# First block of a fused attention and mixture-of-experts kernel: a list order for its attention, half-slot conversion, another ring for one buffer

## The chip, the core and the metric

The kernel runs on one core of a Trainium2 chip. The metric is device time in microseconds of one execution; three executions of the kernel before are at hand, and one more was profiled. Engines are called PE (TensorE), DVE (VectorE), ACT (ScalarE), POOL (GpSimd) and SP (SyncE, which only issues the DMAs here).

## The reference

What is computed, cut to what matters (B, H, S, D = 8, 8, 576, 64; 4608 tokens of 512 features; 2048 hidden features; 8 experts):

```python
q_s = softmax(q, axis=-1); k_s = softmax(k, axis=2)          # k: over the sequence
kv  = einsum('bhsd,bhse->bhde', k_s, v)
x   = einsum('bhsd,bhde->bhse', q_s, kv)                     # -> x[4608, 512]
r   = maximum(x @ w_in, 0); x = (s * r * r + b) @ w_out      # w_in, w_out arrive as 8-byte floats
out = gate(x) * (relu(x @ w1[e]) @ w2[e])                    # e: each token's best expert
```

## The kernel before

The kernel has two parts. The first runs over 12 blocks of 384 tokens (index t) and within a block over 16 slots (index m). Slot m of block t issues the first product of 128 hidden features (`emit_l1`, lines 426 to 428, 12 matmuls, called L1), the activation of the slot before (`emit_g`, on ACT), and the second product of two slots before (`emit_l2`, called L2). Block 0 alone does L2 in full precision for all but its last two slots (L462), reading the joined weight; later products use a high and a low part (L464 to L466). The second part of the kernel is the expert product over sorted tokens; nothing in it is touched.

Two kinds of other work are woven into the slots as Python generators, one step of each per half slot: before L1 (first half) and after L2 (second half).

The attention. A K job (`attn_k`) takes one batch and one pair of heads: maxima over the sequence on DVE (L218 to L225), a transpose on PE (L229), a reduction on DVE (L232), a transpose on PE that spreads it (L235), a subtraction on DVE (L254, L256), Exp on ACT (L261, L262), ten matmuls with v on PE (L270), the division on DVE (L276 to L278), and a high and a low part of the result (`kvh` on ACT, L284; `kvl` on DVE, L287). A Q job (`attn_q`) takes one block and one pair of heads: row maxima on DVE (L298), six Exp on ACT (L333 in block 0, L364 in block 1), the division on DVE (L337 to L340), three transposes on PE (L347), a copy on ACT (L349), the output matmul with `kv` on PE (L352), and a high part on ACT (`xth`, L355) and a low part on DVE (`xtl`, L356). Each job of block 0 ends in loading (through SP) the data of the job that will use its buffers next: k and v at the division, q at `xth`.

The weights. The two weight matrices arrive as 8-byte floats in 16 pairs of 128-row groups of 1 MB each, in the order in0, in1, out0, in2, out1, ... in7, out6, out7. `conv_load` issues a pair's two DMAs; `conv_a` scales the upper words on ACT (Abs, L147) and takes the lowest bits and the sign on DVE (L148, L149); `conv_b` joins them on DVE (L156) and writes the high part on ACT (L160); `conv_c` subtracts on DVE (L164). The joined pair lives in a ring of two buffers for each matrix (`cxin`, `cxout`), `ct` has one buffer, and L462 reads the joined pair of w_out directly. `conv_step` does, in one go: the load of pair i+4, `conv_b` of pair i-1, `conv_a` of pair i, `conv_c` of pair i-1.

What sets the order. The program runs under a manual schedule: each engine executes its instructions in the order in which the Python code issues them, and waits are put in by the framework. Ahead of slot 0 there are 16 head steps (`for c in range(-16, 0)`), in each of which every active job advances by one step; `plan_k` and `plan_q` hold the half slot at which each job starts, and `conv_step` runs at head steps -16 and -7. In block 0, `conv_step` runs ahead of L1, twice in slot 0. PSUM has three rings: `ps_h` (2 banks, L1), `ps_y` (3 banks, L2) and `ps_a` (3 banks, all of the attention). SP issues loads in program order as well.

The loads ahead of the head are issued in this order (w is one weight pair, k, q and v the four head pairs of block 0):

```python
for w in "q0 k0 w k1 q1 q2 v0 k2 v2 k3 q3 v1 w v3 w".split():
```

Of the kernel before, what the change touches and what calls it, by code (L numbers as in the profile page):

```python
# [11 lines left out]
I32 = mybir.dt.int32  # L12
# [13 lines left out]
NM = DFF // 128  # L26
# [10 lines left out]
KP = 1  # L37
# [5 lines left out]
def attn_ffn_moe(ctx: ExitStack, tc: tile.TileContext, q, k, v, w_in, w_out, s_in, b_in,  # L43
                 emb, tau, w1, w2, out, ysc=None):
# [23 lines left out]
    def ps_a():  # L68
        return ps.tile([128, 512], F32, tag="a", name="ps_a", bufs=3)
# [69 lines left out]
    def conv_a(kind, i):  # L139

        t = sp.tile([128, 1024], I32, tag="ct", name="ct", bufs=1)
        x = sp.tile([128, 1024], I32, tag="cx" + kind, name="cx" + kind)
        raw = raw_t.pop((kind, i)).rearrange("p n c -> p (n c)")
        r = raw.rearrange("p (f two) -> p f two", two=2)
        r16 = raw.bitcast(U16).rearrange("p (f four) -> p f four", four=4)
        x16 = x.bitcast(U16).rearrange("p (f two) -> p f two", two=2)
        nc.scalar.activation(out=t.bitcast(F32), in_=r[:, :, 1].bitcast(F32), func=AF.Abs, scale=2.0 ** -112)  # L147
        nc.vector.tensor_scalar(out=x, in0=r[:, :, 0], scalar1=29, scalar2=None, op0=ALU.logical_shift_right)  # L148
        nc.vector.tensor_scalar(out=x16[:, :, 1], in0=r16[:, :, 3], scalar1=0x8000, scalar2=None,  # L149
                                op0=ALU.bitwise_and)  # L150
        conv_t[kind, i] = (t, x)
# [61 lines left out]
    def attn_k(b, j, kt, vt, dg, after=None, ke=None):  # L213
# [11 lines left out]
        nc.vector.tensor_tensor(out=d2[0:64], in0=d2[0:64], in1=k4[0:64, :, 4, :], op=ALU.max)  # L225
        yield
        if b <= KP:
            pt = ps_a()
            nc.tensor.transpose(pt[:, 0:128], dg, ident)  # L229
# [3 lines left out]
            yield  # L233
            pb = ps_a()
            nc.tensor.transpose(pb[:, 0:128], cm.to_broadcast([128, 128]), ident)  # L235
# [20 lines left out]
        nc.vector.tensor_tensor(out=k4[0:64, :, 4, :], in0=k4[0:64, :, 4, :], in1=mb[0:64], op=ALU.subtract)  # L256
        if b > KP:
            yield
# [5 lines left out]
        if b > KP:  # L264
            yield
        pk = ps_a()
        for r in range(5):
# [16 lines left out]
        nc.scalar.activation(out=kvh[b % 2][:, j, :], in_=dg, func=AF.Copy)  # L284
        if b > KP:
            yield
# [14 lines left out]
    def attn_q(t, j, qt, after=None, qe=None):  # L301
        i = t % 2
# [25 lines left out]
        elif t == 0:  # L328
# [6 lines left out]
            yield  # L335
            yield
            nc.vector.tensor_scalar(out=qr, in0=qr, scalar1=1e-9, scalar2=None, op0=ALU.add)  # L337
# [8 lines left out]
            for r in range(NC):  # L346
# [7 lines left out]
            after()  # L354
            nc.scalar.activation(out=xth[0][:, j, :], in_=px[:, 0:BT], func=AF.Copy)  # L355
            nc.vector.tensor_tensor(out=xtl[0][:, j, :], in0=px[:, 0:BT], in1=xth[0][:, j, :].bitcast(F32),  # L356
                                    op=ALU.subtract)
# [483 lines left out]
    with tc.manual_schedule():  # L841
# [10 lines left out]
        for i in range(NP):  # L852
            if i + 1 < NP:
# [4 lines left out]
                 "v": lambda j: load_v(0, j, v0[j])}  # L858
        for w in "q0 k0 w k1 q1 q2 v0 k2 v2 k3 q3 v1 w v3 w".split():
            if w == "w":  # L860
                conv_load(*loads.pop(0))
            else:
                load0[w[0]](int(w[1]))
        nc.sync.dma_start(out=s_sb, in_=s_in.partition_broadcast(128))
        nc.sync.dma_start(out=b_sb, in_=b_in.partition_broadcast(128))
        conv_load(*loads.pop(0))
        conv_i = [0]

        def conv_step():

            i = conv_i[0]
            if i >= len(order) + 1:
                return
            if loads:
                conv_load(*loads.pop(0))
            if i > 0:
                conv_b(*order[i - 1])
            if i < len(order):
                conv_a(*order[i])
            if i > 0:  # L880
                conv_c(*order[i - 1])
            conv_i[0] += 1

# [9 lines left out]
        for j in range(4):  # L893
            plan_k.append((2 * j - 16, 0, j, k0[j], v0[j], d0[j]))
            plan_q.append(((0, 2, 4, 7)[j] - 16, 0, j, q0[j]))
        for b, sl in enumerate(((-4, 4, 12, 22), (28, 40, 52, 63), (75, 87, 98, 109), (120, 132, 144, 156),
                                (168, 180, 191, 203), (216, 228, 240, 252), (264, 276, 287, 299)), start=1):
            for j in range(4):
                plan_k.append((sl[j], b, j, kt_s, vt_s, dg_s))
        for j, sl in enumerate((-2, 6, 12, 22)):  # L900
            plan_q.append((sl, 1, j, qt_s))
# [25 lines left out]

        for c in range(-16, 0):
            start_pairs(c)
            run(act)  # L930
            if c in (-16, -7):
                conv_step()
        start.close()
# [74 lines left out]
        for t in range(NB):  # L1008
            for m in range(NM + (LAG if t == NB - 1 else 0)):
# [13 lines left out]
                if t == 0:  # L1023
                    next(g, None)
                    conv_step()
                    if m == 0:
                        conv_step()
                step(prep)
# [7 lines left out]
                if m < NM:  # L1036
                    start_pairs(2 * (NM * t + m) + 1)
                run(act)
                if (t, m) == (0, NM - 1):
                    assert conv_i[0] >= len(order) + 1  # L1040
                    consts_late()
                    late_open()
# [139 lines left out]
```

## Time and profile before

| | us |
|---|---|
| median of three runs (lowest, highest) | 1409.32 (1408.02, 1411.92) |
| profiled execution | 1407.17 |
| its span, first to last instruction | 1405.4 |
| busy in the span: PE, DVE, ACT, POOL | 1338.8, 1008.0, 889.4, 173.1 |
| mean granted clock of PE, share of full speed | 0.983 |

The page's shares of busy time are means over the whole span. The change concerns the first tenth of it, so the views to read are those by stretch: windows with each engine's busy time, the waits (who waited for whom, and for how long), and the timeline, whose rows give start and length of each instruction and in brackets how long its engine stood idle ahead of it and what released it.

### The profile page before, as it was taken

What the parts mean: (1) busy time and instruction counts of PE and PEld (TensorE: products, weight loads), DVE (VectorE), ACT (ScalarE), POOL (GpSimd) and SP (SyncE); (2) the same over time, 40 slices, a digit from 0 to 9 for tenths busy, and PEclk for the clock granted to TensorE, in tenths of its full rate; (3) what the DMA queues carried; (4) which work ended last, traced back from release to release, by engine and by line L of the source; (5) the groups of instructions that cost most, each with busy time, mean ns of one, the idle gap of its engine ahead of it and who ended that gap; (6) DMA issues with size and microseconds to landing.
All of it is one profiled execution on the core that took longest, in us unless ns stands there. A gap on an engine that the chain in (4) does not pass through costs nothing. (4 is left out here: it accounts for less than half of the span.)

```text
span 1405.4 us, 22783 instructions
## 1 busy us (share of the span) xinstructions
PE 1338.8 (95%) x7650; PEld 1181.1 (84%) x7650; DVE 1008.0 (72%) x2589; ACT 889.4 (63%) x1767; POOL 173.1 (12%) x170
## 2 busy tenths in 40 slices
PE   4898999999999999999999999998999999999995
PEld 2666888888888889888989988987888989899994
DVE  6886797878696969596969593647777666666642
ACT  5776767777676776677777675664554555555542
POOL 0000000000000000000010100113533221212110
PEclk9899999999999999999999999999999999999998
DMA  8641412121211121212111000412222222523332
GB/s 274 221 164 31 124 38 51 37 56 29 57 40 51 30 68 29 51 29 63 35 46 29 27 20 15 159 38 61 68 64 65 69 69 73 190 69 129 128 110 73
DMA packets 107456, 104.72 MB, mean 75 GB/s; under 512 B 55105, under 2 KB 83521, under 8 KB 107331
## 3 DMA queue, kind: packets, MB, share of 16 engines
q1 hardware_dynamic: 100098, 83.74, 20.3%
q0 software_dynamic: 7232, 19.44, 4.2%
q8 instruction: 62, 1.02, 0.3%
q14 instruction: 64, 0.52, 0.2%
HBM read 141.07 MB, written 19.73 MB: 114 GB/s over the span
## 5 line engine op out<-in xcount | busy, mean ns | idle before, releaser
L426 PE MATMUL ps_h<-xth,win 128*128 128x384 f32 x768 | 266.8, 347 | 0.8 <-ACT r L439 0.8
L427 PE MATMUL ps_h<-xtl,win 128*128 128x384 f32 x768 | 261.1, 340 | 0.0
L428 PE MATMUL ps_h<-xth,win 128*128 128x384 f32 x768 | 260.8, 340 | 0.0
L465 PE MATMUL ps_y<-wout,gl 128*128 128x512 f32 x534 | 210.9, 395 | 1.1 <-DVE gl L449 1.1
L466 PE MATMUL ps_y<-wout,gh 128*128 128x512 f32 x534 | 211.6, 396 | 0.0
L464 PE MATMUL ps_y<-wout,gh 128*128 128x512 f32 x534 | 210.0, 393 | 0.0
L654 DVE TENSOR_TENSOR l<-r,h 128x1024 fp32r<-128x1024 f32 x143 | 174.5, 1238 | 20.1 <-ACT h L653 17.4
L541 DVE CUSTOM_DVE_ANT_0 scr<-ysb,eb 128x512 bf16<-128x512 f32 x264 | 181.7, 688 | 5.8
L690 PE MATMUL ps_h<-xh,l 128*128 128x256 f32 x576 | 166.5, 289 | 7.5 <-DVE l L654 7.4
L449 DVE TENSOR_TENSOR gl<-r,gh 128x384 fp32r<-128x384 f32 x178 | 97.9, 550 | 100.9 <-ACT gh L447 98.9
L688 PE MATMUL ps_h<-xh,h 128*128 128x256 f32 x576 | 165.4, 287 | 2.6 <-ACT xh L664 1.8
L689 PE MATMUL ps_h<-xh,h 128*128 128x256 f32 x576 | 165.5, 287 | 1.1 <-DVE xh L665 1.1
L653 ACT ACTIVATE h<-r 128x1024 fp32r<-128x1024 f32 x152 | 155.7, 1050 | 0.0
L426 PEld LDWEIGHTS ps_h<-xth,win 128*128 128x128 f32 x768 | 145.6, 190 | 9.2 <-ACT r L439 1.6
L427 PEld LDWEIGHTS ps_h<-xtl,win 128*128 128x128 f32 x768 | 145.6, 190 | 5.3 <-issue 0.5
L428 PEld LDWEIGHTS ps_h<-xth,win 128*128 128x128 f32 x768 | 145.4, 189 | 0.0
L439 ACT ACTIVATE r<-ps_h 128x384 f32<-128x384 f32 x192 | 93.7, 488 | 80.5 <-PE ps_h L428 69.3
L446 ACT ACTIVATE r<-r,b_sb,s_sb 128x384 f32<-128x384 f32 x178 | 126.3, 709 | 5.9
L705 DVE SCALAR_TENSOR_TENSOR hl<-ps_h,hh 128x512 fp32r<-128x512 f32 x76 | 52.5, 691 | 104.5 <-ACT hh L704 94.0
L704 ACT ACTIVATE hh<-ps_h 128x512 fp32r<-128x512 f32 x76 | 45.4, 597 | 129.4 <-PE ps_h L690 117.1
L690 PEld LDWEIGHTS ps_h<-xh,l 128*128 128x128 f32 x576 | 112.7, 196 | 9.8 <-DVE l L654 9.8
L466 PEld LDWEIGHTS ps_y<-wout,gh 128*128 128x128 f32 x534 | 100.3, 188 | 23.0
(264 smaller groups left out, 2505.3 us busy)
## 6 DMA issues: line engine op xcount, KB each, us to landing
r<-moe_w SPq DMA_DIRECT2D x156, 512.0 KB
ysc<-ysb SPq DMA_DIRECT2D x36, 256.0 KB
x<-xr SPq DMA_DIRECT2D x288, 32.0 KB
qt_s<-q SPq DMA_DIRECT2D x45, 192.0 KB
rawin<-moe_w_in SPq DMA_DIRECT2D x16, 512.0 KB
rawout<-moe_w_out SPq DMA_DIRECT2D x16, 512.0 KB
kt_s<-k SPq DMA_DIRECT2D x29, 256.0 KB
vt_s<-v SPq DMA_DIRECT2D x29, 256.0 KB
```

The source lines that it names most:

```text
L426: nc.tensor.matmul(hp, wh[:, ws], xth[i][:, kk, :], start=(kk == 0), stop=False)
L427: nc.tensor.matmul(hp, wh[:, ws], xtl[i][:, kk, :], start=False, stop=False)
L428: nc.tensor.matmul(hp, wl[:, ws], xth[i][:, kk, :], start=False, stop=(kk == KC - 1))
L464: nc.tensor.matmul(y, g[:, cs], wh, start=(m == 0), stop=False)
L465: nc.tensor.matmul(y, l[:, cs], wh, start=False, stop=False)
L466: nc.tensor.matmul(y, g[:, cs], wl, start=False, stop=(m == NM - 1))
L541: nc.vector.tensor_tensor_reduce(out=junk_box[-1], in0=yt, in1=eb[:, e, :], scale=1.0, scalar=0.0, op0=ALU.mult, op1=ALU.add, accum_out=dt ...
L653: nc.scalar.activation(out=hi, in_=raw, func=AF.Copy)
L654: (eng or nc.vector).tensor_tensor(out=lo, in0=raw, in1=hi.bitcast(F32), op=ALU.subtract)
L688: nc.tensor.matmul(o, wh, xh[:, kk, :], start=(kk == 0), stop=False)
L689: nc.tensor.matmul(o, wh, xl[:, kk, :], start=False, stop=False)
L690: nc.tensor.matmul(o, wl, xh[:, kk, :], start=False, stop=(kk == KC - 1))
```

## The change

- The head is no longer 16 rounds over all jobs, but one list that names, entry by entry, the job whose next step is issued: k0 to k3 and q0 to q3 of block 0, c (a generator that converts in0), K and Q (the first jobs of the next batch and block, begun in the list), and w (a weight load). Two steps of K and two of Q are issued in the list, where four and two were issued in the head before.
- For the list, the jobs of block 0 get further `yield`s, so that each step of theirs is on one engine: between subtraction and Exp, and between `kvh` and `kvl` in `attn_k`, between `xth` and `xtl` in `attn_q`, where also an empty step goes.
- The K jobs of block 0 take their PSUM banks from `ps_y`, which L2 doesn't use yet; Q stays on `ps_a`.
- The first loads are in another order, with the first weight pair behind q2 instead of behind k0, the second one last; the third and fourth are issued in the list.
- `conv_step` is cut into two halves. The first, ahead of L1, issues the load and `conv_b`; the second, behind the slot's second attention step, issues `conv_a` of the next pair and `conv_c`. A pair is finished one slot later than before.
- The joined pair out7 gets its buffer from the ring of w_in.
- Some jobs of later batches and blocks start at other half slots.

```diff
     def conv_a(kind, i):
...
-        x = sp.tile([128, 1024], I32, tag="cx" + kind, name="cx" + kind)
+        room = "in" if (kind, i) == ("out", NM // 2 - 1) else kind
+        x = sp.tile([128, 1024], I32, tag="cx" + room, name="cx" + kind)
...
+        bank = ps_y if b == 0 else ps_a
         if b <= KP:
-            pt = ps_a()
+            pt = bank()
...
-            pb = ps_a()
+            pb = bank()
...
-        if b > KP:
+        if b > KP or b == 0:
             yield
         e = kt if ke is None else ke()
...
-        pk = ps_a()
+        pk = bank()
...
         nc.scalar.activation(out=kvh[b % 2][:, j, :], in_=dg, func=AF.Copy)
-        if b > KP:
+        if b > KP or b == 0:
             yield
...
             yield
-            yield
             nc.vector.tensor_scalar(out=qr, in0=qr, scalar1=1e-9, scalar2=None, op0=ALU.add)
...
             nc.scalar.activation(out=xth[0][:, j, :], in_=px[:, 0:BT], func=AF.Copy)
+            yield
...
-        for w in "q0 k0 w k1 q1 q2 v0 k2 v2 k3 q3 v1 w v3 w".split():
+        for w in "q0 k0 k1 q1 v0 k2 q2 w v1 k3 q3 v2 v3 w".split():
...
-        conv_load(*loads.pop(0))
-        conv_i = [0]
-
-        def conv_step():
+        conv_i = [1]
+
+        def conv_first():
+            yield
+            conv_a(*order[0])
+            yield
+            conv_b(*order[0])
+            yield
+            yield
+            conv_c(*order[0])
+
+        def conv_step(half):
 
             i = conv_i[0]
-            if i >= len(order) + 1:
+            if i > len(order):
                 return
-            if loads:
-                conv_load(*loads.pop(0))
-            if i > 0:
-                conv_b(*order[i - 1])
-            if i < len(order):
-                conv_a(*order[i])
-            if i > 0:
-                conv_c(*order[i - 1])
-            conv_i[0] += 1
+            if half == 0:
+                if loads:
+                    conv_load(*loads.pop(0))
+                if i > 1:
+                    conv_b(*order[i - 1])
+            else:
+                if i < len(order):
+                    conv_a(*order[i])
+                if i > 1:
+                    conv_c(*order[i - 1])
+                conv_i[0] += 1
...
-            plan_k.append((2 * j - 16, 0, j, k0[j], v0[j], d0[j]))
-            plan_q.append(((0, 2, 4, 7)[j] - 16, 0, j, q0[j]))
-        for b, sl in enumerate(((-4, 4, 12, 22), (28, 40, 52, 63), (75, 87, 98, 109), (120, 132, 144, 156),
+            plan_k.append((-16, 0, j, k0[j], v0[j], d0[j]))
+            plan_q.append((-16, 0, j, q0[j]))
+        for b, sl in enumerate(((-2, 6, 14, 22), (30, 41, 52, 63), (75, 87, 98, 109), (120, 132, 144, 156),
...
-        for j, sl in enumerate((-2, 6, 12, 22)):
+        for j, sl in enumerate((-2, 6, 14, 22)):
...
-        for c in range(-16, 0):
-            start_pairs(c)
-            run(act)
-            if c in (-16, -7):
-                conv_step()
+        start_pairs(-16)
+        line = {f"{w}{j}": act[4 * i + j] for i, w in enumerate("kq") for j in range(4)}
+        line["c"] = conv_first()
+        act.clear()
+        start_pairs(-2)
+        line["K"], line["Q"] = act
+        for w in ("q0 q0 k0 k1 k0 k0 k1 q0 k0 k0 q0 q0 k1 q1 k0 k1 k2 q1 k0 k1 k2 k2 k1 q2 k2 q1 q2 k2 q1 k0 c q2 "
+                  "k1 q1 k3 q2 k2 q0 c q2 k3 q0 w w k2 k0 q3 c q3 k3 k1 c q3 k3 q1 k1 k3 q3 q1 c k3 q3 k3 k2 q0 k2 k3 "
+                  "q2 q1 k3 q2 k0 K q3 q3 q2 K q3 Q Q k1 k2 k3").split():
+            if w == "w":
+                conv_load(*loads.pop(0))
+            else:
+                next(line[w], None)
...
+        conv_step(0)
+        conv_step(1)
...
                 if t == 0:
                     next(g, None)
-                    conv_step()
-                    if m == 0:
-                        conv_step()
+                    conv_step(0)
...
                 run(act)
+                if t == 0:
+                    conv_step(1)
```

## Rows read from the trace of the kernel before

**Rows 1.** Windows by stage: us, busy us (instructions) by engine, granted clock, DMA share, rate.

```profile
core 0: us, PE busy (x) PEld busy (x) DVE busy (x) ACT busy (x) POOL busy (x), PEclk, DMA share, GB/s
...
4.76:40.08 35.32, 18.89 (x110) 10.99 (x111) 24.95 (x71) 20.16 (x72) 0.00 (x0) 0.87 0.96 308
40.08:58.46 18.38, 15.12 (x73) 12.55 (x74) 17.08 (x29) 13.56 (x29) 0.00 (x0) 0.79 0.76 257
58.46:102.99 44.53, 42.11 (x208) 29.41 (x207) 38.30 (x64) 36.65 (x78) 1.11 (x4) 1.00 0.47 157
102.99:135.34 32.35, 27.52 (x123) 19.42 (x122) 21.65 (x47) 20.37 (x43) 3.14 (x7) 0.95 0.13 34
135.34:1405.40 1270.06, 1235.12 (x7144) 1108.67 (x7142) 906.02 (x2381) 798.64 (x1548) 166.84 (x144) 0.99 0.22 63
```

**Rows 2.** Waits of PE, 40 to 136 us: total, times, longest.

```profile
PE ps_a L270 <- ACT kt_s L261: 5.6, 2, 4.8
PE ps_a L235 <- DVE cm L232: 2.8, 2, 1.6
PE ps_a L379 <- DVE qt_s L371: 2.4, 1, 2.4
```

**Rows 3.** Timeline of the head: start, length, engine, line, operands [idle before <-releaser].

```profile
2.63 1.06 SPq L136 DMA_DIRECT2D rawin<-moe_w_in  x2
...
5.76 0.54 DVE L298 TENSOR_REDUCE qs<-qt_s 128x6 f32<-128x384 f32 x1
...
8.79 1.28 ACT L147 ACT_TABLE_LOAD   x1 [8.79 <-DMA rawin<-moe_w_in]
8.81 0.69 DVE L148 TENSOR_SCALAR cxin<-rawin 128x1024 int32<-128x1024 int32 x1 [2.51 <-DMA rawin<-moe_w_in]
...
10.08 1.13 ACT L147 ACTIVATE ct<-rawin 128x1024 f32<-128x1024 f32 x1
...
11.11 0.34 ACT L333 ACTIVATE qt_s<-qt_s,qs 128x64 f32<-128x64 f32 x1
```

**Rows 4.** The same view: lengths of single steps of block 0's attention.

```profile
13.23 0.17 DVE L337 TENSOR_SCALAR qr<-qr 128x6 f32<-128x6 f32 x1 [1.21 <-ACT qt_s L333]
...
14.28 0.90 PE L347 MATMUL ps_a<-ident,qe 128*128 128x128 f32 x3 [2.19 <-DVE qe L340]
...
15.80 1.56 PE L270 MATMUL ps_a<-vt_s,ke 128*64 128x66 f32 x20 [0.62 <-ACT ke L261]
...
18.50 1.62 PE L352 MATMUL ps_a<-qt_s,dg_s 128*128 128x384 f32 x2 [0.52 <-DVE dg_s L278]
...
20.24 0.28 DVE L287 TENSOR_TENSOR kvl<-dg_s,kvh 128x128 fp32r<-128x128 f32 x1
...
39.14 0.56 DVE L356 TENSOR_TENSOR xtl<-ps_a,xth 128x384 fp32r<-128x384 f32 x1 [1.70 <-ACT xth L355]
```

**Rows 5.** The same view: one weight pair's conversion on DVE.

```profile
27.91 1.22 DVE L156 SCALAR_TENSOR_TENSOR cxin<-ct,cxin 128x1024 int32<-128x1024 int32 x1
...
29.04 0.69 DVE L148 TENSOR_SCALAR cxin<-rawin 128x1024 int32<-128x1024 int32 x1
...
29.76 0.76 DVE L149 TENSOR_SCALAR cxin<-rawin 128x1024 uint16<-128x1024 uint16 x1
...
30.41 1.21 DVE L164 TENSOR_TENSOR win<-cxin,win 128x1024 fp32r<-128x1024 f32 x1
```

**Rows 6.** Timeline of PE and DVE, 115 to 127 us.

```profile
115.33 2.74 PE L462 MATMUL ps_y<-cxout,gh 128*128 128x512 f32 x6
...
118.11 0.69 DVE L148 TENSOR_SCALAR cxout<-rawout 128x1024 int32<-128x1024 int32 x1 [5.72 <-PE ps_y L462]
...
122.89 1.45 PE L270 MATMUL ps_a<-vt_s,kt_s 128*64 128x66 f32 x20 [4.83 <-ACT kt_s L261]
...
125.29 0.52 PE L427 MATMUL ps_h<-xtl,win 128*128 128x384 f32 x1
...
126.54 0.34 PE L428 MATMUL ps_h<-xth,win 128*128 128x384 f32 x1
```

More of the change, by code (lines that the diff above doesn't have):

```diff
@@ L926, in start_pairs @@
                     act.append(attn_q(t, j, qt, after=aft, qe=e))
-        for c in range(-16, 0):
-            start_pairs(c)
-            run(act)
-            if c in (-16, -7):
-                conv_step()
+        start_pairs(-16)
[11 more added lines that the diff above has]
+                next(line[w], None)
+        assert all(next(line[w], 0) == 0 for w in line if w not in "KQ")
+        conv_step(0)
+        conv_step(1)
         start.close()
@@ L1038, in attn_ffn_moe @@
                 run(act)
+                if t == 0:
+                    conv_step(1)
                 if (t, m) == (0, NM - 1):
-                    assert conv_i[0] >= len(order) + 1
+                    assert conv_i[0] > len(order)
                     consts_late()
```

## The prediction

> **What bounds the kernel now.** I read the windows by stage first [rows 1]. Their bounds are the starts of PE's L426 in slots 0, 3, 11 and 16 of the first token block (slot 16 is slot 0 of the second block), which I call L1(0), L1(3), L1(11), L1(16). From L1(16) to the end PE is busy 1235.12 of 1270.06 us: that part is bound by PE, the change doesn't touch its instructions, and it moves as a whole with the moment at which it begins. So the question is by how much L1(16), now at 135.34, moves. Before it PE is not the bound: up to L1(0) at 40.08 it has 18.89 us of work, and DVE has 24.95 us of work in a stretch of 35.32, so that DVE is idle for 10.37. In slots 3 to 10 PE is busy 42.11 of 44.53 us (5.57 a slot) with DVE close behind (38.30). In slots 11 to 15 it falls back: 27.52 of 32.35, or 6.47 a slot.
>
> Then the waits of PE between L1(0) and L1(16) [rows 2]: the longest is 4.83 us, at L270 for the exponentials of a K job. Its row [rows 6] leads back to DVE: the first step of the last weight pair (L148, out7) waited 5.72 us for the L2 matmuls that end with the row at 115.33, because its buffer was still that of out5; everything behind it in DVE's order, the attention too, waited with it. PE then came back at 1.2 GHz: a matmul of L1 lasts 0.52 us at 125.29 and 0.34 at 126.54.
>
> Last, the head in order of time [rows 3]. The row maxima of q0 end at 6.30, but the first Exp starts at 11.11: ACT stood in order behind the Abs of in0, whose megabyte was in SP's queue ahead of k1, behind its table load, and behind the Abs itself. DVE lost 2.51 us there in the same way.
>
> **The change, part by part.** No arithmetic instruction is added or removed; only orders, banks and one buffer change. I sum against the profiled execution (1407.17 us, of which 1405.4 is the span); the median, 1409.32, lies 2.15 above it, and I carry the difference over.
>
> *The head (list order, loads, own banks).* DVE's work ahead of L1(0) is 24.95 less what now comes behind it: the first two steps of in1 (0.69 + 0.76 [rows 5]), the row maxima of the next Q (0.54, priced by L298 [rows 3]), three low halves of kv (3 x 0.28 [rows 4]), and one maximum of the next K (0.28, by the same row as the nearest of its size): 21.84. The maxima of q0 (0.54) can run while k0 is still landing, so DVE ends at 4.76 + 21.30 + its waits = 26.1 + waits. Both ends for the waits: 2 us (an estimate: the last chain of output matmul, copy and difference, which nothing can cover; now it shows as the 1.70 wait of the last xtl [rows 4]) and 10.4 as now, which gives L1(0) between 28 and 36.5. Between them I stepped through the list by hand, each engine taking its steps in list order at the lengths of [rows 3 to 5]: Exp of q0 from 5 to 7 (after 1.28 of table load), kv matmuls (L270, 1.56 each) of the four pairs at 10.8, 16.2, 20.8 and 27.0, the output matmuls (L352, 1.62 each) at 18.7, 22.9, 28.5 and 30.1, one transpose, and L1(0) at 32.2. DVE's largest waits on the way are 1.4 (maximum of k2, whose transpose is behind the kv matmuls of pair 0 on PE), 2.4 (product of q3, whose exponentials are on ACT behind the copy of in0) and 0.7 (last difference); all of them together 6.1. I take 32.2: **7.9 us earlier**. In0 doesn't decide there: with 4.2 MB ahead (tile sizes) and the 308 GB/s of the window [rows 1] everything has landed by about 18, and its first use is at 18.0.
>
> *SP's queue.* The loads of out0 and in2 now stand behind the loads for the next K and Q, and these wait for kv matmul 0 and output matmul 0 (20.3 above). Two more megabytes at 308 GB/s land by 28; their first steps come at 38 and 43. Nothing is late by 10 us; cost zero, and if that cover were gone each us of lateness would cost one.
>
> *K and Q of the next block, two steps less in the head.* The maximum and the second transpose of K move into slot 0, where PE has no L2 yet: nothing on the path. Stepping on from 32.2, L1(1) and L1(2) start at 36.5 and 44.4 and L1(3) at 50.3, 18.1 after L1(0) against 18.38 now: **-0.3**.
>
> *Half slots.* The step that joins the two parts of a weight (L156) now stands at the head of a slot and waits for an Abs issued half a slot before; behind it in DVE's order stand the second half's attention steps, the next pair's shift and mask, and the difference L164. In slots where six Exp (11.11 to 13.23, 2.1 us [rows 3, 4]) stand ahead of the Abs on ACT, L156 waits about 1.3; elsewhere the waits of L156 and L164 go under. The trace has no such order, so I bound it: as now, 5.57 a slot (8 slots: 0), or by stepping, 23.0 us for each four slots, 5.74 a slot (8 slots: **+1.4**). Below nothing is possible too: PE idles 2.42 us in these slots [rows 1], and all of it could go. I take +0.5, nearer to the row. A weight is ready a slot later than now; in the stepping the joined out pair is there 1.9 us before the L2 that reads it and the in pair 3 us before L1, so the cover is thin, and this is a rival below.
>
> *out7 in the other ring.* Its buffer was last read by the difference of in6, three slots earlier. The 5.72 on DVE and the 4.83 on PE go, and the five slots 11 to 15 take 5.57 to 5.74 each, 27.9 to 28.7 instead of 32.35: **-3.6 to -4.5**, I take -4. Late next there is K's exponential at its normal pace. The table's fill (POOL, L118 on) now waits for the difference of out7 instead of L156; it is read much later.
>
> Sum: 7.9 + 0.3 - 0.5 + 4.0 = 11.7 us earlier. 1407.17 - 11.7 = 1395.5 for a profiled execution, **1397.6** beside the median.
>
> One rule speaks against a larger gain. The row: after the 4.83 us wait PE runs at 1.2 GHz [rows 6], and the granted clock is 0.79 over slots 0 to 2 [rows 1]. The Trainium skill, "TensorE: Matmul & The Clock Gate" (What's actually happening), says that the slow clock is the default and that activity releases it. By that rule the head, where PE is still fed in pieces, ends at 1.2 GHz and L1(0) is as slow as now; without it L1(0) would be faster by 12 x (0.52 - 0.34), about 2.2 us. My steps have the slow lengths.
>
> **The rivals.**
> 1. *The head keeps its waits.* The chains K to Q to output are as long as now, and DVE waits about as much (10.4), or the small transfers land later than I assume. For: each pair still passes DVE, PE, ACT in turn seven or eight times. Against: the 4.8 us at the start of [rows 3] go whatever follows. L1(0) at 36.5, sum -7.4: 1402.
> 2. *The conversion becomes the bound.* With one slot less of lead, PE waits for L156 or L164. If each of 16 slots costs 0.5 more, 8 us go back: 1406, no change that can be told (a measurement here tells some 0.3%, 4.2 us). Against: DVE has 6.2 us to spare in slots 3 to 10.
> 3. *Slower.* In the slots, L156 waits for the whole Abs (1.13) and L164 for the whole copy (taken as long) in every slot, since DVE takes its steps in order and can't go round either. That is 2.3 us a slot, of which the stepping has about half; another 1.1 in 16 slots is 18 us: 1415. It decides from a slot of 6.5 us on. Against: now the same chain runs in one piece, with both waits in the same half, and slots 3 to 10 take 5.57.
> 4. *More.* DVE's waits in the head fall to 2 us and the slots close up to PE's work: 4 + 2.4 more, 1391.
> 5. *The list brings nothing,* L1(0) stays at 40 behind the transfers, and only out7 counts: 1405. The 308 GB/s speaks against it; I count it with 2.
>
> **How the numbers follow.** Forecast (1394 to 1400.5) 0.60; rival 1 (1401 to 1405) 0.19; rivals 2 and 5 0.09; rival 3 0.04; rival 4 0.08. Faster by over 0.3% holds forecast, 1 and 4: 0.87; within 0.3%: 0.09; slower 0.04. The range goes from 1392 (a part of rival 4) to 1404 (most of rival 1), leaving about 0.2 out.
>
> **What would show it.** L1(0) near 32 and the first Exp before 7; no wait of L148 for ps_y; PE's waits between L1(0) and L1(16) below 5 us; L1(16) between 122 and 126. Wrong if L1(0) lies beyond 36, if slots 3 to 10 take more than 48 us in all, if PE's L426 waits for L164 or L462 for L156, or if PE gets idle time after L1(16) that it doesn't have now.

## The result and the profile after

| | before | changed kernel |
|---|---|---|
| median, us (lowest, highest, executions) | 1409.28 (1408.02, 1411.92) | 1395.84 (1395.08, 1398.78, 4) |
| ratio to before, 95% interval | | 0.9906 (0.9886 to 0.9926) |
| profiled execution, us; its span | 1407.17; 1405.4 | 1398.78; 1397.1 |

The change makes the kernel 13.4 us faster; the forecast was 1397.6 in a range of 1392 to 1404. The total came out right. Of its terms only the head's did so for the reason given, and that only up to L1(0).

First the windows by stage, as in [rows 1] (columns as there), cut at the same places: PE's first row of L1 in slots 0, 3 and 11 of block 0, and slot 0 of block 1. In the changed kernel the lines are one or two further down: L428 is the first line of L1, L464 the L2 of block 0, L272 the matmuls of a K job.

```profile
4.82:31.92 27.10, 18.41 (x109) 10.98 (x110) 21.08 (x62) 17.06 (x69) 0.00 (x0) 1.00 0.90 269
31.92:51.35 19.43, 14.13 (x74) 11.81 (x73) 16.37 (x31) 13.89 (x30) 0.00 (x0) 0.82 0.73 263
51.35:95.57 44.22, 42.75 (x208) 29.50 (x207) 37.96 (x64) 35.38 (x75) 0.00 (x0) 1.00 0.60 213
95.57:124.06 28.49, 26.42 (x124) 17.79 (x122) 23.38 (x43) 21.25 (x45) 4.62 (x10) 1.00 0.21 64
124.06:1397.10 1273.04, 1236.71 (x7142) 1110.11 (x7142) 908.50 (x2392) 799.11 (x1550) 169.80 (x144) 0.99 0.22 63
```

Against [rows 1]: L1(0) comes 8.2 us earlier (40.08 to 31.92), slots 0 to 2 take 1.05 more (18.38 to 19.43), slots 3 to 10 take 0.3 less, slots 11 to 15 take 3.9 less (32.35 to 28.49), and L1(16) comes 11.3 earlier (135.34 to 124.06). The rest, in which the change only starts one K job half a slot later, took 3.0 more in this execution (1270.06 to 1273.04), and so the profiled execution, the highest of the four, is only 8.4 below the one before. Those 3 us have a section of their own at the end.

The head, in order of time (start, length, engine, line, operands, in brackets the idle time ahead and what ended it). These rows answer to [rows 3] and [rows 4]:

```profile
3.37 1.28 ACT L335 ACT_TABLE_LOAD   x1 [3.37 <-DMA qt_s<-q]
4.67 0.35 ACT L335 ACTIVATE qt_s<-qt_s,qs 128x64 f32<-128x64 f32 x1
...
11.06 1.56 PE L272 MATMUL ps_y<-vt_s,ke 128*64 128x66 f32 x20 [0.64 <-ACT ke L263]
...
17.16 1.56 PE L272 MATMUL ps_y<-v,ke 128*64 128x66 f32 x20 [1.49 <-DMA v<-v]
...
18.09 0.42 DVE L219 TENSOR_TENSOR scr<-k 128x256 f32<-128x256 f32 x1 [0.88 <-DMA k<-k]
...
25.23 0.17 DVE L338 TENSOR_SCALAR qr<-qr 128x6 f32<-128x6 f32 x1 [2.26 <-ACT q L335]
...
31.92 0.67 PE L428 MATMUL ps_h<-xth,win 128*128 128x384 f32 x1
```

The reader is to see that the first Exp no longer stands behind in0 (4.67 instead of 11.11) and brings its table load forward with it (3.37 instead of 8.79), and that two loads are late all the same: the second v by 1.49 on PE, a k by 0.88 on DVE.

Then the waits of PE, from L1(0) to L1(16), and the longest of DVE from 0 to 124 us (line waiting, what for, total, times, longest):

```profile
PE ps_a L272 <- ACT kt_s L263: 5.6, 3, 4.5
PE ps_h L428 <- ACT r L441: 2.4, 3, 0.9
PE ps_a L237 <- DVE cm L234: 0.8, 1, 0.8
```

```profile
DVE cxin L157 <- ACT ct L148: 5.3, 4, 1.4
DVE wout L165 <- ACT wout L161: 3.8, 5, 0.8
```

PE's largest wait is again one for K's exponential, but at another place: the 4.83 of [rows 6] at the end is gone, and 4.47 stand in slot 1. The subtraction that Exp needs (L256) comes on DVE right behind a conversion's last step (L165).

```profile
40.23 1.21 DVE L165 TENSOR_TENSOR win<-cxin,win 128x1024 fp32r<-128x1024 f32 x1
...
41.36 0.67 DVE L256 TENSOR_TENSOR kt_s<-kt_s,ps_a 128x512 f32<-128x512 f32 x1
42.07 0.63 ACT L263 ACTIVATE kt_s<-kt_s 128x512 f32<-128x512 f32 x1 [1.89 <-DVE kt_s L256]
42.75 1.56 PE L272 MATMUL ps_a<-vt_s,kt_s 128*64 128x66 f32 x20 [4.47 <-ACT kt_s L263]
...
45.27 0.52 PE L429 MATMUL ps_h<-xtl,win 128*128 128x384 f32 x1
```

Behind this wait PE runs at 1.2 GHz again (0.52 for a matmul of L1, 0.34 at 2.4 GHz).

### The profile page after: what moved, and what is told of

Read it like the earlier page. It is cut to its first block, busy times and chain, and to the rows that moved or that the text cites. A ratio compares the mean times of both kernels' runs of the same rounds, so it can differ in the third digit from the quotient of the medians.

```text
span 1397.1 us, 22791 instructions
## 1 busy us (share of the span) xinstructions
PE 1338.4 (96%) x7650; PEld 1180.2 (84%) x7650; DVE 1007.8 (72%) x2589; ACT 888.1 (64%) x1767; POOL 176.4 (13%) x170
## 5 line engine op out<-in xcount | busy, mean ns | idle before, releaser
L428 PE MATMUL ps_h<-xth,win 128*128 128x384 f32 x768 | 265.9, 346 | 2.4 <-ACT r L441 2.4
L656 DVE TENSOR_TENSOR l<-r,h 128x1024 fp32r<-128x1024 f32 x143 | 174.4, 1237 | 19.7 <-ACT h L655 17.0
L428 PEld LDWEIGHTS ps_h<-xth,win 128*128 128x128 f32 x768 | 145.7, 190 | 11.2 <-ACT r L441 4.3
L468 PEld LDWEIGHTS ps_y<-wout,gh 128*128 128x128 f32 x534 | 100.3, 188 | 22.9
```

The lines of the kernel that those rows point to most:

```text
L428: nc.tensor.matmul(hp, wh[:, ws], xth[i][:, kk, :], start=(kk == 0), stop=False)
L468: nc.tensor.matmul(y, g[:, cs], wl, start=False, stop=(m == NM - 1))
L656: (eng or nc.vector).tensor_tensor(out=lo, in0=raw, in1=hi.bitcast(F32), op=ALU.subtract)
```

## Experiments

The question was which part of the change brought the 11.3 us, and whether the parts add. The changed kernel has three: the **head** (list, loads, banks, fewer steps of K and Q), the **half slots** (which are two things: one conversion less in slot 0, so that each pair is finished a slot later, and the cut of the step into two), and the **ring** of out7. Kernels were made with one part alone, with one part taken back, and with single edits inside a part.

All of them in one table. "0 to 3" is the time from L1(0) to L1(3), and so on, from the timeline of PE in each kernel's profiled execution. Ratios are to the kernel before, whose medians beside these runs were 1408.58 (first four), 1407.67 (next four) and 1407.57 (last four).

| kernel | median, us (lowest to highest, n) | ratio (95%) | L1(0) | 0 to 3 | 3 to 11 | 11 to 16 | L1(16) |
|---|---|---|---|---|---|---|---|
| before | 1409.28 | 1 | 40.1 | 18.4 | 44.5 | 32.3 | 135.3 |
| changed | 1395.84 (1395.08 to 1398.78, 4) | 0.9906 (0.9886 to 0.9926) | 31.9 | 19.4 | 44.2 | 28.5 | 124.1 |
| e1 changed, ring taken back | 1394.55 (1393.01 to 1399.67, 6) | 0.9910 (0.9894 to 0.9927) | 30.4 | 20.0 | 43.9 | 28.7 | 123.0 |
| e2 before, ring alone | 1405.41 (1401.75 to 1407.28, 11) | 0.9974 (0.9965 to 0.9983) | 40.7 | 19.5 | 44.7 | 26.8 | 131.6 |
| e3 before, half slots alone | 1400.85 (1400.23 to 1402.47, 5) | 0.9948 (0.9936 to 0.9961) | 40.5 | 13.2 | 44.9 | 27.7 | 126.4 |
| e4 before, head alone | 1407.29 (1403.8 to 1409.48, 12) | 0.9989 (0.9979 to 0.9999) | 31.7 | 22.6 | 45.1 | 33.6 | 133.0 |
| e5 changed, K on `ps_a` | 1397.27 (1394.81 to 1402.95, 6) | 0.9923 (0.9906 to 0.9940) | 33.9 | 19.8 | 43.9 | 27.9 | 125.6 |
| e6 changed, old load order | 1400.92 (1397.58 to 1402.26, 6) | 0.9949 (0.9934 to 0.9963) | 34.7 | 19.7 | 44.0 | 28.3 | 126.8 |
| e7 changed, K's four steps in the list | 1396.52 (1396.03 to 1398.5, 6) | 0.9922 (0.9910 to 0.9935) | 33.8 | 16.0 | 44.0 | 28.6 | 122.3 |
| e8 changed, in0 loaded later | 1395.84 (1394.26 to 1396.79, 5) | 0.9912 (0.9898 to 0.9926) | 31.0 | 19.0 | 44.7 | 28.3 | 122.9 |
| e9 before, one conversion less in slot 0 | 1402.75 (1399.62 to 1403.1, 5) | 0.9962 (0.9947 to 0.9977) | 41.4 | 13.4 | 46.0 | 29.9 | 130.6 |
| e10 head and e9's edit, uncut | 1398.84 (1394.73 to 1401.59, 6) | 0.9937 (0.9921 to 0.9952) | 30.6 | 19.0 | 45.0 | 29.9 | 124.5 |
| e11 e7, e8 and one list entry | 1391.42 (1388.36 to 1395.08, 5) | 0.9884 (0.9865 to 0.9903) | 30.7 | 14.4 | 45.6 | 28.3 | 119.0 |
| e12 changed, again | 1394.24 (1393.83 to 1396.42, 4) | 0.9901 (0.9883 to 0.9918) | 31.5 | 19.4 | 44.3 | 28.2 | 123.3 |

The changed kernel, e1, e4, e10 and e12 have the same head (list, loads and banks); their L1(0) lie between 30.4 and 31.9. They follow PE's wait for the second v: 30.4 where it waits for none (e1), 30.6 with 0.5 (e10), 31.5 to 31.9 with 1.5 to 1.6 (e12, e4, changed). So a difference of 1.5 us in L1(0) between two profiles can't be told from none, and one of that size in L1(16) is not relied on here either.

### The ring, taken back and alone

```diff
-        room = "in" if (kind, i) == ("out", NM // 2 - 1) else kind
-        x = sp.tile([128, 1024], I32, tag="cx" + room, name="cx" + kind)
+        x = sp.tile([128, 1024], I32, tag="cx" + kind, name="cx" + kind)
```

The lines marked - stand in the changed kernel; e1 is the changed kernel with the line marked +, e2 the kernel before with the lines marked -.

> The changed kernel with out7's joined pair back in the ring of w_out; nothing else differs. The prediction's theory (the ring takes away the 5.72 us wait, worth 4 us): 4 us slower than the changed kernel, some 1400, with L148/L149's step of out7 waiting about 5 us for L2 matmuls, and L1(16) near 128. Rival theory (the half-slot order issues that step behind the L2 that frees the buffer, one slot later than before, so the ring is not needed): within 1 us of the changed kernel, no wait of that step for ps_y over 0.5 us, L1(16) at 124 to 125.

> The kernel before, with only out7's joined pair moved to the ring of w_in. The prediction's theory: 4 us faster than before (1405), the 5.72 us wait on DVE and the 4.83 us wait on PE gone, L1(16) at 130.5 to 131.7. Rival: the wait only moves to another wait of DVE or ACT in the same slots (the conversion still ends where attention makes it end), and less than 1.5 us is gained, L1(16) beyond 133.8.

Taken back, nothing returns: e1 is as fast as the changed kernel (0.9910 and 0.9906), its slots 11 to 15 take 28.7. Alone, it does what the prediction priced: slots 11 to 15 fall from 32.3 to 26.8, L1(16) comes 3.7 earlier (in this profile L1(0) and slots 0 to 2, where out7 plays no part yet, took 1.7 more), the time falls by 3.2 us by the medians. The rows of out7's first steps (DVE, `cxout<-rawout`) and of the L2 that last reads out5, whose buffer out7 takes in the ring of w_out (PE), first of e1:

```profile
107.24 2.74 PE L463 MATMUL ps_y<-cxout,gh 128*128 128x512 f32 x6
...
109.96 1.21 DVE L156 SCALAR_TENSOR_TENSOR cxout<-ct,cxout 128x1024 int32<-128x1024 int32 x1
...
111.09 0.68 DVE L148 TENSOR_SCALAR cxout<-rawout 128x1024 int32<-128x1024 int32 x1
```

and of e2, where the lines are one further down on DVE:

```profile
114.12 0.69 DVE L149 TENSOR_SCALAR cxout<-rawout 128x1024 int32<-128x1024 int32 x1
...
117.15 2.74 PE L463 MATMUL ps_y<-cxout,gh 128*128 128x512 f32 x6
```

In e2 out7 begins 3 us before that L2 does (it runs until 119.89): there the other ring is needed. In e1 it begins 1.1 us after the L2 has ended (107.24 + 2.74 = 109.98) and waits for nothing, in the old ring. With the half slots DVE comes to out7 only after that L2 is done. So the 5.72 us of [rows 6] can be removed in two ways, and the change has both; the second is worth nothing.

### The half slots, alone

```diff
-        def conv_step():
+        def conv_step(half):
...
+            if half == 0:
+                if loads:
+                    conv_load(*loads.pop(0))
+                if i > 0:
+                    conv_b(*order[i - 1])
+            else:
+                if i < len(order):
+                    conv_a(*order[i])
+                if i > 0:
+                    conv_c(*order[i - 1])
+                conv_i[0] += 1
...
-                    conv_step()
-                    if m == 0:
-                        conv_step()
+                    conv_step(0)
...
+                if t == 0:
+                    conv_step(1)
```

> The kernel before with only the conversion cut into half slots (head as before, out7 in its own ring, a pair finished one slot later than before). The prediction's theory: slots 3 to 10 get 0 to 1.4 us longer and the end keeps its wait, so 1409 to 1411. Rival (the half-slot order frees the end by itself): the 5.72 us wait is gone, 3 to 5 us faster than before, 1404 to 1406, L1(16) at 130 to 132.

This part, which had been priced at a cost of 0.5, is the largest gain of all: 7.7 us by the medians, L1(16) 9.0 earlier. That is more than either of the two theories had. 5.2 are in slots 0 to 2 (18.38 to 13.20) and 4.6 in slots 11 to 15 (32.35 to 27.73), where out7's wait is gone as in e1; L1(0) and slots 3 to 10 took 0.8 more. What happened in slots 0 to 2 is to be seen in the timeline of the kernel before:

```profile
45.34 1.22 DVE L156 SCALAR_TENSOR_TENSOR cxout<-ct,cxout 128x1024 int32<-128x1024 int32 x1
...
47.84 1.22 DVE L164 TENSOR_TENSOR wout<-cxout,wout 128x1024 fp32r<-128x1024 f32 x1
...
49.41 0.56 DVE L371 TENSOR_TENSOR qt_s<-qt_s,qr 128x384 f32<-128x384 f32 x1
...
50.02 0.55 PE L379 MATMUL ps_a<-ident,qt_s 128*128 128x128 f32 x3 [2.41 <-DVE qt_s L371]
...
51.90 0.52 PE L427 MATMUL ps_h<-xtl,win 128*128 128x384 f32 x1
```

and of e3:

```profile
43.38 0.56 DVE L371 TENSOR_TENSOR qt_s<-qt_s,qr 128x384 f32<-128x384 f32 x1
...
47.95 0.49 PE L379 MATMUL ps_a<-ident,qt_s 128*128 128x128 f32 x3
48.20 0.42 PE L426 MATMUL ps_h<-xth,win 128*128 128x384 f32 x1
```

The window of slots 0 to 2 in e3, columns as in [rows 1]:

```profile
40.51:53.71 13.20, 13.20 (x74) 11.15 (x74) 12.21 (x23) 10.87 (x26) 0.00 (x0) 1.00 0.51 143
```

Before, a whole conversion (45.34 to 49.06) stands on DVE ahead of the product L371 that PE's transposes wait for. PE loses 2.41 there, and the slot after it runs at 1.2 GHz (0.52 at 51.90). In e3 the same product begins at 43.38, PE waits for nothing there and keeps 2.4 GHz. In the window PE is now busy all the time: of the 5.18 us, 3.26 were idle time (15.12 busy of 18.38) and 1.92 work that took longer at the lower clock. The wait is in [rows 2] (L379, 2.4), with its line and what it waited for, and the prediction went past it.

### One conversion less in slot 0, without the cut

```diff
                     conv_step()
-                    if m == 0:
-                        conv_step()
```

> The kernel before without the second whole conversion step in slot 0, so that every pair is finished one slot later, as in the changed kernel, but still in one piece ahead of L1. Theory A (the half slots win by this lag alone: slot 0 has 3.8 us of DVE work less in front of the attention, and out7's first step is issued a slot later): L1(3) at 53 to 55 as in the half-slot run, L1(16) at 126 to 128.5, 1400 to 1403. Theory B (it is the cut that wins, because the attention's steps come between the two parts): L1(3) at 57 or later, out7's step still waits 2 us or more, L1(16) beyond 131, 1405 or more.

Of the two things in the half slots this is the one that makes slots 0 to 2 short: 13.4, as in e3 (13.2). At the end out7's wait is gone too, since out7 now comes a slot later. What the cut adds to that is to be seen in the later slots: 46.0 and 29.9 here against 44.9 and 27.7 with it, 1.1 and 2.1 us, and so L1(16) is at 130.6, beyond the 128.5 of theory A. In the time the two are not told apart (1402.75 and 1400.85, the intervals overlap).

### The head, alone and with that edit

e4 is the changed kernel with out7 in its own ring and both halves of the conversion run in one go ahead of L1, twice in slot 0, as before:

```diff
                     conv_step(0)
+                    conv_step(1)
+                    if m == 0:
+                        conv_step(0)
+                        conv_step(1)
...
-                if t == 0:
-                    conv_step(1)
```

> The changed kernel's head (list order, banks of its own, order of the first loads, start slots of the jobs), with the conversion in whole steps as before and out7 in its own ring. The prediction's theory: L1(0) near 32 and L1(3) 8 us earlier than before, the 5.7 us wait at out7 as before, so 8 us faster than before: 1401. Rival (the earlier start only makes PE wait longer at out7 or in the slots, because DVE's conversion sets the end of block 0): 3 us faster or less, 1406 or more, L1(16) beyond 132.

The head alone brings L1(0) from 40.1 to 31.7, and the kernel 1.3 us by the medians (0.9989, 0.9979 to 0.9999): almost all is given back. Slots 0 to 2 take 22.6 instead of 18.4, slots 11 to 15 have out7's wait as before (33.6). The timeline of e4 behind L1(0):

```profile
37.77 0.69 DVE L148 TENSOR_SCALAR cxout<-rawout 128x1024 int32<-128x1024 int32 x1
...
40.28 1.21 DVE L156 SCALAR_TENSOR_TENSOR cxout<-ct,cxout 128x1024 int32<-128x1024 int32 x1
...
42.76 1.22 DVE L164 TENSOR_TENSOR wout<-cxout,wout 128x1024 fp32r<-128x1024 f32 x1
...
44.80 0.68 DVE L255 TENSOR_TENSOR kt_s<-kt_s,ps_a 128x512 f32<-128x512 f32 x1
...
46.20 1.57 PE L271 MATMUL ps_a<-vt_s,kt_s 128*64 128x66 f32 x20 [8.10 <-ACT kt_s L262]
```

K's subtraction (L255), two steps further back in the job than before, now stands behind two conversions on DVE, and PE waits 8.10 for its Exp. Without the second conversion in slot 0 (e10):

> The changed kernel's head with the conversion in one piece, without the second step in slot 0, out7 in its own ring: the head-only run with the lag. Theory A (lag alone): the 8.1 us wait for K's exponential in slot 1 falls by 3 us or more, L1(3) at 51 to 52, L1(16) at 124 to 126, 1396 to 1399, as the changed kernel. Theory B (the cut): L1(3) at 53.5 or later, L1(16) beyond 128, 1402 or more.

slots 0 to 2 take 19.0, K's wait is 4.5, L1(16) is at 124.5 and the time 1398.84: by the ratios 0.5% less than e4, some 7 us. So the head is worth little by itself and more beside the lag. At L1(16): head alone -2.35 (e4 against before), beside the lag -6.1 (e10 against e9), beside the half slots -3.4 (e1 against e3). Half slots alone are -9.0 (e3), both -12.4 (e1), where the sum of the two alone would be -11.3; that excess of 1.1 is within what equal heads differ by.

### K's four steps back in the list

```diff
-                  "q2 q1 k3 q2 k0 K q3 q3 q2 K q3 Q Q k1 k2 k3").split():
+                  "q2 q1 k3 q2 k0 K q3 q3 q2 K q3 Q Q K K k1 k2 k3").split():
```

> The changed kernel with two more steps of K (maximum and second transpose) at the end of the list, as many as the head issued before. Theory A (the 4.47 us wait of PE in slot 1 for K's exponential, and the 1.2 GHz stretch after it, come from issuing K two steps later): the wait falls below 1.5 us, L1(0) starts up to 1 us later, L1(3) at 47 to 49 instead of 51.4, 2.5 to 4 us faster. Theory B (DVE's work sets slots 0 to 3 whatever the order): L1(3) no earlier than 50.4, less than 1 us gained.

PE's waits from 33 to 136 us in e7:

```profile
PE ps_h L428 <- ACT r L441: 4.2, 4, 1.8
PE ps_a L237 <- DVE cm L234: 1.6, 1, 1.6
PE ps_a L272 <- ACT kt_s L263: 1.2, 2, 0.6
```

The 4.5 us at L272 are gone, as theory A said; but PE waits 1.8 more for the activation (L428), L1(0) comes 1.8 later than in the changed kernel, slots 0 to 2 take 16.0 instead of 19.4, and L1(16) comes 1.7 earlier, near the 1.5 that equal heads differ by. In the time no gain is told (1396.52 against 1395.84 and 1394.24), where theory A had 2.5 to 4 us.

### The loads

```diff
-        for w in "q0 k0 k1 q1 v0 k2 q2 w v1 k3 q3 v2 v3 w".split():
+        for w in "q0 k0 w k1 q1 q2 v0 k2 v2 k3 q3 v1 w v3".split():
```

> The changed kernel with the first loads in the order of before (in0's megabyte behind k0, v1 and v3 last). Theory A (the transfers decide the start of the head): k1's maxima 3 us later, v1 later than now, L1(0) at 34 to 36, 2 to 4 us slower. Theory B (what cost time before was in0's Abs ahead of the exponentials in ACT's order, which the list has changed): L1(0) less than 1 us later, time within 1 us.

With the weight pair ahead of k1, the maxima of k1 wait 4.8 us for their load on DVE (waits of DVE, 4 to 40 us):

```profile
DVE scr L219 <- DMA k<-k: 4.8, 1, 4.8
```

L1(0) is at 34.7, 2.8 later than in the changed kernel, and the time is 5 to 7 us longer (1400.92), the only one of the single edits inside the head that the time shows. Its profile, one of its two shortest executions (1397.62), accounts for 2.7 at L1(16); where the rest is lost was not seen. The other way, with in0 behind v1 and k3:

```diff
-        for w in "q0 k0 k1 q1 v0 k2 q2 w v1 k3 q3 v2 v3 w".split():
+        for w in "q0 k0 k1 q1 v0 k2 q2 v1 k3 w q3 v2 v3 w".split():
```

> The changed kernel with in0's load behind v1 and k3 instead of ahead of them. Theory A (the waits of PE for v1, 1.49 us, and of DVE for k3, 0.88 us, come from in0's megabyte ahead of them): both waits below 0.3 us, L1(0) 1 to 2 us earlier (30 to 31). Theory B (in0's own steps then wait for its landing, at 19 to 21): L148 waits 1 us or more for in0, L1(0) within 0.5 us.

L1(0) is at 31.0 and the time 1395.84. PE waits 0.6 for v and DVE 0.6 for a k, where theory A had both below 0.3; in e1 and e10, with in0 in its place, the two waits are none and 0.6, 0.5 and 0.5. All this lies within what equal heads differ by. That in0's megabyte is what makes v1 and k3 late is not shown.

### The banks

```diff
-        bank = ps_y if b == 0 else ps_a
+        bank = ps_a
```

> The changed kernel with the K jobs of block 0 on ps_a again, so that K and Q share three banks. Theory A (banks matter little: the kernel before shows no wait for a shared bank over 0.6 us): L1(0) within 1 us of the changed kernel (31 to 33), time within 1 us. Theory B (in the list the output matmul of pair 0 holds its bank from 19 to 29 us, until its low part is taken, and three banks are then too few): PE waits 2 to 4 us in the head, L1(0) at 34 to 36, 2 to 4 us slower than the changed kernel.

Waits of PE in the head, 8 to 34 us:

```profile
PE ps_a L353 <- DVE k L258: 2.8, 1, 2.8
```

An output matmul of Q waits 2.8 until a K job's subtraction has read its bank, and L1(0) comes at 33.9, 2.0 later than in the changed kernel and beyond the range of equal heads (30.4 to 31.9), if just short of the 34 of theory B. In the time (1397.27) it is not told apart from the changed kernel.

### Together

e11 is the changed kernel with K's four steps (e7), in0 loaded later (e8), and the join of in0 one entry later in the list, behind q3's Exp, for which DVE waited 2.26 us at 25.23:

```diff
-                  "k1 q1 k3 q2 k2 q0 c q2 k3 q0 w w k2 k0 q3 c q3 k3 k1 c q3 k3 q1 k1 k3 q3 q1 c k3 q3 k3 k2 q0 k2 k3 "
-                  "q2 q1 k3 q2 k0 K q3 q3 q2 K q3 Q Q k1 k2 k3").split():
+                  "k1 q1 k3 q2 k2 q0 c q2 k3 q0 w w k2 k0 q3 q3 c k3 k1 c q3 k3 q1 k1 k3 q3 q1 c k3 q3 k3 k2 q0 k2 k3 "
+                  "q2 q1 k3 q2 k0 K q3 q3 q2 K q3 Q Q K K k1 k2 k3").split():
```

> The changed kernel with K's two further steps in the list, in0's load behind v1 and k3, and in0's joining step behind q3's exponentials in the list. If the three gains add up (1.8 and 1.2 us at L1(16) in the runs of each, and some 1 us for q3's product, which now waits 2.3 us): L1(0) at 32 to 33, L1(16) at 119.5 to 121, 3 to 4 us faster than the changed kernel. If slots 0 to 3 are bound by DVE's and ACT's work instead: L1(16) at 122 or later and no more than 2 us gained.

Waits of PE from 31 to 136 us:

```profile
PE ps_h L428 <- ACT r L441: 4.4, 5, 1.7
PE ps_a L272 <- ACT kt_s L263: 1.8, 3, 0.6
```

L1(0) is at 30.7 in spite of the two steps more, slots 0 to 2 take 14.4, L1(16) is at 119.0 (119.5 to 121 had been expected). The time is 1391.42, 0.9884 of before, the fastest of all the kernels here. The changed kernel beside it, once more:

> The changed kernel once more, unaltered, beside the three others. Every theory: L1(16) at 123 to 125 and 1394.5 to 1397. If the profile shows no 1.2 GHz stretch at the 1.5 us waits for K's exponentials beyond slot 16, the span behind L1(16) should be near 1270 us, not the 1273 of the first profile of this kernel; with two such stretches 1273.

It has 1394.24, and L1(16) at 123.3; behind that it took 1271.3 us, for which 1273 had been expected. e11 is 2.8 us below it by the medians, and their intervals (0.9865 to 0.9903, 0.9883 to 0.9918) overlap a little. At L1(16) e11 is 4.3 earlier, which is more than equal kernels differ by.

## Point by point

- **Head, -7.9: right up to L1(0), and by its steps.** L1(0) at 31.92 (32.2 said), DVE busy for 21.08 and idle for 6.02 in the head's window (21.30 and 6.1 said), Exp of q0 at 4.67 ("from 5 to 7"), kv matmuls at 11.06, 17.16, 20.97 and 27.64 (10.8, 16.2, 20.8 and 27.0), output matmuls at 19.34, 23.11 and 29.13 (18.7, 22.9, then 28.5), DVE's wait before q3's product 2.26 (2.4). Two steps inside it were off. "Everything has landed by about 18" is too early: PE waited 1.49 for v at 17.16 and DVE 0.88 for k at 18.09; the bytes were counted, but the order of the landings, in which v1 and k3 stand behind the megabyte of in0, was not weighed (whether that is the cause is open, as e8 shows). And the banks had no price: they are worth 2.0 at L1(0) (e5).
- **K and Q two steps less, "nothing on the path": wrong.** It was reasoned from PE, which has no L2 yet in slot 0. But the step that is late is on DVE, where the subtraction stands behind the conversion: 4.47 at L272, and a slot at 1.2 GHz behind it. Slots 0 to 2 took 1.05 more instead of 0.3 less. e7 shows it: with the steps back in the list the wait is gone. The wait is there without the cut too (4.5 in e10).
- **Half slots, +0.5: the step that failed.** It was costed only on slots 3 to 10, and there it was near enough (-0.3; the waits of L157 are four, the longest 1.4, as stepped: "about 1.3"). Left out was what the diff also says: slot 0 no longer converts twice. That is 5 us in slots 0 to 2 when it stands alone (e9), and at the end the lag of a slot takes out7's wait away too.
- **out7, -4: right as a size, wrong as a cause.** Slots 11 to 15 took 28.49 (27.9 to 28.7 said), and the ring alone does take the wait (e2). But in the changed kernel the wait is gone without it (e1). The ring and the half slots were priced as if each had its own wait; they share one. The prediction had the means to see it: it stepped the half slots, and could have stepped out7 in them.
- **The sum.** 11.3 at L1(16) for 11.7 said. With the half slots first, then the head, then the ring, the experiments give 8.9 (e3), 3.4 (126.4 to 123.0, e1) and nothing (124.1 and 123.3 with the ring). So the total was right by luck, because two errors met: the half slots' gain in slots 0 to 2 was left out (5.2), and about as much is lost there by the head, which makes these slots 6.2 longer than in e3 (19.43 against 13.20; 3.5 of that go with K's two steps, e7). The head's 8 us at L1(0) were taken to arrive whole at L1(16); beside the half slots 3.4 of them did.
- **The clock in the head.** L1(0) begins with matmuls of 0.67, 0.52, 0.52, 0.52 and 0.44 and is at 0.34 from the sixth on; the forecast had the slow length in all twelve, as in the kernel before. From the first to the start of the twelfth it takes 2.76 instead of 3.67 us, so the faster part is worth 0.9. By the rule of the Trainium skill cited there, "TensorE: Matmul & The Clock Gate" (What's actually happening), the slow clock is the default and activity releases it; the trace agrees, with the release at the sixth matmul and not behind the twelfth.
- **Rivals.** 1 fell with L1(0) at 31.92. 2 and 3 have their mechanism in the trace, 5.3 us of waits of L157 and 3.8 of L165, but the eight slots take 44.2: the waits are covered. 4 fell, since the one wait for q3's exponentials alone is 2.26. That e11 is at the 1391 named for rival 4 doesn't bear it out: its L1(0) is at 30.7, where the rival had 28. 5 fell with L1(0).
- **Signs said ahead.** No wait of out7 for `ps_y`, first Exp before 7, L1(16) in 122 to 126: all seen. "PE's waits between L1(0) and L1(16) below 5": wrong, 8.8, of which 4.47 are K's. Of the signs of being wrong the last was seen, in small: PE is idle for 36.3 us behind L1(16) instead of 34.9, of which one wait for DVE at 186.72 is 1.16; the kernel before has none over 0.3 of that kind. Why is open.

## What to carry to other kernels

Time that an early stage gains arrives at the end only if the engine that feeds the next stage is early too: a head 8.35 us shorter brought 2.35 at the end of the block while DVE still had two conversions to do ahead of K (e4), and one 10.7 us shorter brought 6.1 where DVE had one to do (e10 against e9). When a change has several parts, step each wait through all of them together: two edits may remove the same wait, and then one is worth nothing. And read every wait of the stage for what stands ahead of its releaser on that engine: the 2.41 at L379, with the slot at 1.2 GHz behind it, was most of the 5.2 us that the half slots gained in slots 0 to 2.

## What was unexpected of the hardware

The part behind L1(16), whose instructions are those of before except for the start of one K job, took from 1267.3 us (e9) to 1275.6 (e5) in the profiled executions. A part of that is the clock. At one place of the program PE waits 1.5 us for K's exponential in all fourteen profiles. In the changed kernel:

```profile
506.75 0.95 PE L272 MATMUL ps_a<-vt_s,kt_s 128*64 128x66 f32 x20 [1.47 <-ACT kt_s L263]
507.63 0.44 PE L428 MATMUL ps_h<-xth,win 128*128 128x384 f32 x1
...
508.47 0.52 PE L428 MATMUL ps_h<-xth,win 128*128 128x384 f32 x1
...
513.48 0.34 PE L428 MATMUL ps_h<-xth,win 128*128 128x384 f32 x1
```

and in the kernel before:

```profile
516.74 0.95 PE L270 MATMUL ps_a<-vt_s,kt_s 128*64 128x66 f32 x20 [1.48 <-ACT kt_s L261]
517.62 0.44 PE L426 MATMUL ps_h<-xth,win 128*128 128x384 f32 x1
...
518.26 0.34 PE L426 MATMUL ps_h<-xth,win 128*128 128x384 f32 x1
...
521.94 0.33 PE L426 MATMUL ps_h<-xth,win 128*128 128x384 f32 x1
```

The waits are equal to a hundredth, and the matmuls ahead of them and behind them are the same; yet in one the granted clock falls to 1.2 GHz and a matmul of L1 takes 0.52, in the other it stays at 2.4 and takes 0.34. The windows of the stretch, of the changed kernel (from 507.5) and of the kernel before (from 518.8), with the granted clock third from the end:

```profile
507.50:511.00 3.50, 3.50 (x15) 3.43 (x15) 3.36 (x10) 3.01 (x7) 0.00 (x0) 0.57 0.00 0
```

```profile
518.80:522.30 3.50, 3.50 (x19) 3.10 (x19) 3.33 (x13) 3.06 (x7) 0.00 (x0) 1.00 0.25 58
```

The changed kernel has a second such stretch, at 729 us, with a wait of 1.47 ahead of it. By the rows one stretch costs 1.5 us: from L1 behind the wait to L1 of the next slot it is 5.85 (507.63 to 513.48) in the one and 4.32 (517.62 to 521.94) in the other. Behind L1(16), the profiles with neither have 1267.3 to 1270.1 (before, e1, e4, e6, e9, e10) and, once, 1272.6 (e7); those with one have 1269.8 (e11), 1272.6 (e3) and 1275.6 (e5); those with both 1271.2 to 1273.0 (changed, e2, e8, e12). So the stretches go with some of the spread. e5's 1275.6 goes with a granted clock of 0.95 in the 200 us that begin 800 us behind L1(16), where the kernel before, the changed kernel, e3 and e7 have 0.97; the rest has no cause that was found here. Nor is it known what decides whether the clock falls: e1, which differs from the changed kernel in one buffer, has the same wait, of 1.48 at 505.63, and no slow stretch behind it. What follows is that edits worth 2 us at L1(16) can't be told in the time of these kernels, as e5, e7 and e8 show.

One reading of the view itself: the granted clock of the head's window is 1.00 in the changed kernel, while ten matmuls of K take 1.56 there and 0.95 at 506.75. In the head the lengths, not the column, are what to read: they are the long ones, as at 1.2 GHz.
